# Two attention layers with state-space layers between: last stage of the kernels' transform on 32x32 tiles, loads and weights' loads moved

## The chip, the cores and the metric

One core of a Trainium2 chip. The metric is the device time of one execution in microseconds (us). Engines: PE (TensorE, matmuls and transposes), DVE (VectorE), ACT (ScalarE), POOL (GpSimd), SP (SyncE, which here issues most DMAs). Each engine runs its instructions in the order in which they stand.

## The reference

x has 2048 positions of 640 channels. Two pairs of layers, each behind a layer norm and added to x: attention with 32 heads of 20 channels, then a state-space layer whose long convolution is computed by FFT.

```python
def _A_ref(x, wqkv, wo):                      # attention
    q, k, v = qkv[0], qkv[1], qkv[2]
    p = _softmax(scores, axis=-1)
    ...
def _B_ref(u, log_A_real, A_imag, C_real, C_imag, log_dt, D_skip):
    K = 2.0 * jnp.einsum("dn,dnl->dl", C, P).real
    Kf = jnp.fft.rfft(K, L2)
    Uf = jnp.fft.rfft(u_t, L2)
    y = jnp.fft.irfft(Uf * Kf[None, :, :], L2)[:, :, :L]
    return y + u * D_skip[None, None, :]
```

K does not depend on x. Both state-space layers use the same K, so its transform is made once.

## The kernel before, in words

The program runs in this order: K is computed on the chip and written to DRAM (tensor kd); attention 1; its output projection, with the transform of K among it; state-space layer 1; attention 2; its output projection; state-space layer 2.

**Kernels' transform** (`ktransform`, lines 1029 to 1090). Five units of 128 channels. A unit does this:

1. DMA of kl (128 channels x 2048 positions, 1 MB) on SP; DVE adds the skip weight to one column (kl<-kl,skip).
2. 16 transposes by PE (pkt<-ident,kl, line 1053), four to a PSUM tile; four copies to ktr, half on DVE and half on ACT.
3. 32 fp32 matmuls of 128x128 (pkx<-ktr,e, line 1061; two PE instructions each in the trace), four to a PSUM tile; eight copies to kx1, half on DVE and half on ACT.
4. Eight steps q: four transposes (pkt<-ident,kx, line 1070), one copy by ACT to kxt (two buffers), then, one step behind, one fp32 matmul of 128x512 (pkf<-kxt,f, line 1078, two instructions in the trace). DVE shuffles partitions of pkf into kn0 and into kn1 (STREAM_SHUFFLE kn<-pkf), ACT scales kn1 by sgn. After two steps SP stores kn0 to kha and kn1 to khb, 128x1024 floats each. kn0 and kn1 have one buffer each.

PSUM in this stage: tags T, F, X and mm with two banks each.

**Output projection** (`out_proj`, lines 1092 to 1112). 16 groups s of 128 positions. A group loads otl, casts it to oh (ACT), subtracts to get ol (DVE), and runs 30 matmuls of 128x320 (po, lines 1098 and 1104), after which DVE adds po to x in two halves (x<-x,po) and the layer norm's steps follow. In program order, `weave(1000)` at s == 2 puts the whole transform there; a scheduler then decides how the instructions of the groups and of the transform lie among each other on every engine.

**State-space layer** (from line 1163): psx, pst, psv, psy on PE; ka and kb are loaded from kha and khb, 256 KB each.

**Attention.** For a group g of four heads, a block qb of 512 queries and a step kt of 128 keys, PE makes scores S (line 824), ACT takes the exponential (pt<-S), PE multiplies with V (pa, line 841). Beside it, the projections to q and k of the blocks of later heads run (line 578 and others): `fetch` loads their weights (DMA ws on SP), DVE and ACT empty the results, and SP stores them to DRAM as qs and ks. Loads of kop and qop bring them back for each group; for the next group they are issued at qb == 3, kt == 10. How much projection work must be done by which wave of attention is set by the table AHEAD; a planner (`slot`, `need`) places it.

Of the kernel before, what the change touches and what calls it, by code (L numbers as in the profile page):

```python
# [11 lines left out]
F32 = mybir.dt.float32  # L12
# [72 lines left out]
def mha_s4d_kernel(ctx, tc, x_in, wqkv, wo, lar, aim, cr, ci, ldt, dsk,  # L85
# [29 lines left out]
    kha = dram.tile([P, D // 4, P], F32, name="kha")  # L115
    khb = dram.tile([P, D // 4, P], F32, name="khb")
# [277 lines left out]
    def attention(x, stats):  # L394
# [162 lines left out]
        def jobs():  # L557
# [372 lines left out]
        for g in range(H // 4):  # L930
            need(NEED[g], ("v", g // 2))
            for qb in range(4):
                if g == H // 4 - 1 and qb == 3:
                    if tail is None:
                        need(*every)
                        tail = end_jobs()
                    split, fetch = out_split(tail[-1], 1 if first_layer else 2)
                    first = []
                    later.extend(((plan.pe + 7.0, fetch), (plan.pe + 20.0, lambda: first.append(split(0)))))
                    later.sort(key=lambda e: e[0])  # L940
                pa = [pst("A", [P, 512], F32, tag=f"pa{r}", name=f"pa{r}") for r in range(2)]
                for kt in range(NI):
                    kc, pts = P * (kt % 8), []
                    for j in range(2):
                        pts.append(scores(kop[j][kt // 8], kc, qop[j][qb % 2]))
                        if j:
                            ready.append((plan.act, qb, g, kt, pts, pa))
                        fill(j)
                    if kt == 2:
                        for j in range(2):  # L950
                            if qb == 0:
                                load_k(g, j, 1)
                            if qb < 3:
# [69 lines left out]
    DUP0 = list(range(16)) * 2  # L1023
    DUP1 = list(range(16, 32)) * 2

    def by_channel(x1, i2):
        return x1[:, :, i2].rearrange("p g (s c) -> p s g c", c=4)
# [1 line left out]
    def ktransform():  # L1029

        c = ExitStack()
        c1 = c.enter_context(tc.tile_pool(name="f1", bufs=1))
        c2 = c.enter_context(tc.tile_pool(name="f2", bufs=2))
        e1 = c1.tile([P, NI, 2, P], F32, name="e1")
        sy.dma_start(e1, c_e1.rearrange("p (i r k) -> p i r k", i=NI, r=2))
        f2 = c1.tile([P, P], F32, name="f2")
        sy.dma_start(f2, c_f2)
        sgn = c1.tile([P, 1], F32, name="sgn")
        sy.dma_start(sgn, c_sg)

        skip = c1.tile([P, NCT], F32, name="skip")
        sy.dma_start(skip, dsk)

        def unit_load(b):
            kl = c1.tile([P, L], F32, name="kl")
            sy.dma_start(kl, kd[b * P:b * P + P, :])
            ve.tensor_add(kl[:, 0:1], kl[:, 0:1], skip[:, b:b + 1])
            kt = c1.tile([P, NI, P], F32, name="ktr")
# [7 lines left out]
            x1 = c1.tile([P, 32, NI // 2, 16], F32, name="kx1")  # L1056
            for i2 in range(NI // 2):
                ps = pst("X", [P, 2, 2, P], F32, tag="X", name="pkx")
                for r in range(2):
                    for i in range(2):  # L1060
                        te.matmul(ps[:, r, i, :], e1[:, 2 * i2 + i, r, :], kt[:, 2 * i2 + i, :],
                                  start=True, stop=True)
                (ve.tensor_copy if i2 % 2 else se.copy)(by_channel(x1, i2), ps.rearrange("p r i (g c) -> p (r i) g c", c=4))
                yield
            prev = None
            for q in range(9):
                if q < 8:
                    pt = pst("T", [P, 4, P], F32, tag="T", name="pkt")
# [4 lines left out]
                if prev is not None:  # L1073
                    g0 = b * 32 + 4 * (q - 1)
                    if q % 2:
                        kn = [c1.tile([P, 2, 512], F32, name=f"kn{s}") for s in range(2)]
                    px = pst("F", [P, 512], F32, tag="F", name="pkf")
                    te.matmul(px, f2, prev, start=True, stop=True)  # L1078
# [7 lines left out]
                prev = xt  # L1086
                yield
        for b in range(NCT):
            yield from unit_load(b)
        c.close()  # L1090

    def out_proj(x, woh, wol, split, first, ln):
# [35 lines left out]
    def ssm(x, uh, ul, consts, last):  # L1128
# [19 lines left out]
        with ExitStack() as c:  # L1148
# [29 lines left out]
            def stage2b(b, q, xt):  # L1178
                g0 = b * 32 + 4 * q
                ka = c3.tile([P, 512], F32, name="ka")  # L1180
                kb = c3.tile([P, 512], F32, name="kb")
                sy.dma_start(ka, kha[:, g0:g0 + 4, :].rearrange("p g k -> p (g k)"))
                sy.dma_start(kb, khb[:, g0:g0 + 4, :].rearrange("p g k -> p (g k)"))
# [163 lines left out]
    def seq(x, general):  # L1347

        stats = None
        for n in range(0, len(parts), 2):  # L1350
            with ExitStack() as c:
# [49 lines left out]
def _constants():  # L1401
# [12 lines left out]
        f2[r, :, :, :, o] = np.einsum("ihl,cd->ichld", m.reshape(16, 4, 4), e4)  # L1414
    for s, o, m in ((0, 0, C), (1, 0, S), (0, 1, -S), (1, 1, C)):
        fa[:, s, :, :, o] = np.einsum("hli,cd->hlcid", m.reshape(4, 4, 16), e4)
    f2 = f2.reshape(2, NI // 2, 2, 4, P).transpose(1, 0, 2, 3, 4)
    sg = np.zeros((4, 2, 16, 1))
    sg[:, 0], sg[:, 1] = -1.0, 1.0
# [5 lines left out]
    cs = dict(c_e1=e1.reshape(P, -1), c_eb=eb.reshape(P, -1), c_f2=f2.reshape(P, P), c_sg=sg.reshape(P, 1),  # L1425
              c_fa=fa.reshape(P, -1), c_sel=sel.reshape(P, -1), c_lv=lv, c_id=np.eye(P))
    cs = {n: np.ascontiguousarray(a.astype(np.float32)) for n, a in cs.items()}
    for n, a in (("c_e16", e1), ("c_f16", f2)):
# [41 lines left out]
```

## Time and profile before

| what | value |
|---|---|
| median of 3 runs | 2717.64 us (2716.63 to 2720.64) |
| profiled execution | 2718.84 us |
| its span | 2717.1 us |
| mean granted TensorE clock | 0.991 |
| PE, DVE, ACT, POOL busy | 2534.4, 1477.0, 2337.4, 852.6 us |

A page of the profile gives busy time per engine, the chain of work that ended last, and groups of instructions: line, engine, operation, out<-in, shape, count, then busy time and mean ns of one, then the engine's idle time before them and what ended it. In timelines the columns are start, duration, engine, line, operation, and in brackets the idle time before it with its releaser. A row of windows gives the stretch, its length, and busy time with count for PE, PE's weight loads, DVE, ACT, POOL, then the clock, the share of DMA and GB/s. In the rows of a tile, "590/592/697" are the shortest, median and longest duration in ns, followed by the first and last start.

### The profile page before, as it was taken

The numbers are of one execution on the slowest core, as the hardware profiler recorded it, in microseconds if no ns is written. First come the engines' busy times: TensorE is split into PE (matmuls) and PEld (weight loads), VectorE is DVE, ScalarE is ACT, GpSimd is POOL, SyncE is SP. The second block draws the span as 40 slices with busy tenths as digits, with TensorE's granted clock in tenths as the row PEclk, the third lists the DMA queues.
The fourth block names the chain that finished last, engine by engine and source line by source line (L and its number), as shares of the span: only waits on it lengthen the run. The fifth ranks groups of instructions, "written<-read, shape, count | busy, mean of one in ns | idle before, by whom it ended". The sixth has DMA issues, their size and how long they took to land.

```text
span 2717.1 us, 115609 instructions
## 1 busy us (share of the span) xinstructions
PE 2534.4 (93%) x50944; PEld 1445.2 (53%) x50944; DVE 1477.0 (54%) x3292; ACT 2337.4 (86%) x2762; POOL 852.6 (31%) x1282
## 2 busy tenths in 40 slices
PE   7899999999999988999999999899999998888998
PEld 3445444444444433777886445444445443335988
DVE  7777877778856970577776332232232220003865
ACT  7899999999999999455655899899999999997464
POOL 1132333333333343301670122222223223222376
PEclk9999999999999999999999999999999999999999
DMA  6522222232222232455542111111121112112365
GB/s 214 174 62 75 63 77 64 73 75 61 65 51 59 51 112 87 145 210 194 178 142 67 45 52 52 50 53 46 46 66 35 50 36 61 41 38 80 110 191 161
DMA packets 183153, 238.55 MB, mean 88 GB/s; under 512 B 42737, under 2 KB 128241, under 8 KB 180849
## 3 DMA queue, kind: packets, MB, share of 16 engines
q1 hardware_dynamic: 146304, 184.48, 21.0%
q0 software_dynamic: 36336, 46.59, 7.2%
q8 instruction: 402, 6.59, 1.0%
q14 instruction: 111, 0.90, 0.1%
HBM read 154.90 MB, written 76.03 MB: 85 GB/s over the span
## 4 chain that ended last, share of the span: by engine, by line
ACT 49%; PE 30%; issue 9%; DVE 7%; DMA 4%; POOL 1%; SPq 0%; ACTq 0%; DVEq 0%; POOLq 0%
ACT pt L77 47%; PE pa L841 5%; PE S L824 3%; PE psv L1198 3%; PE po L1104 3%; PE psy L1208 2%; PE m L578 2%; PE psx L1186 2%; PE psx L1163 2%; PE po L1098 1%; PE pst L1173 1%; PE pkf L1078 1%; DMA kop<-ks 1%; PE pv L544 1%; PE pq L730 1%
## 5 line engine op out<-in xcount | busy, mean ns | idle before, releaser
L77 ACT ACTIVATE pt<-S 128x1024 f32<-128x1024 f32 x2048 | 1922.9, 1037 | 46.7 <-PE S L824 37.1
L841 PE MATMUL pa<-pt,V 64*32 64x512 f32 x16384 | 1101.0, 590 | 0.9 <-DVE oc L77 0.8
L824 PE MATMUL S<-qop,kop 61*32 61x512 f16 x16384 | 880.4, 381 | 125.4 <-ACT pt L77 105.1
L824 PEld LDWEIGHTS <-kop 61*32 61x32 f16 x16384 | 375.1, 89 | 784.1 <-issue 660.0
L841 PEld LDWEIGHTS pa<-pt,V 64*32 64x32 f32 x16384 | 315.0, 106 | 69.9 <-DVE oc L77 6.6
L77 POOL DMA_DIRECT2D dn<-oc x256 | 126.7, 501 | 700.9 <-DVE oc L77 644.7
L77 DVE COPY oc<-pa 128x512 f32<-128x512 f32 x64 | 44.2, 690 | 312.1 <-PE pa L841 307.2
L77 DVE TENSOR_SCALAR qc<-m 128x512 f32<-128x512 f32 (+1 forms) x68 | 46.9, 689 | 296.4 <-PE m L578 296.4
L77 POOL DMA_DIRECT2D db<-dn x256 | 130.0, 513 | 111.6 <-DMA dn<-dr 107.7
L578 PE MATMUL m<-xh,wh 64*32 64x512 f16 x2560 | 146.7, 379 | 1.4 <-DVE qc L77 1.4
L578 PE MATMUL m<-xh,wl 64*32 64x512 f16 x2560 | 147.3, 378 | 0.0
L578 PE MATMUL m<-xl,wh 64*32 64x512 f16 x2560 | 145.5, 377 | 0.0
L77 POOL DMA_DIRECT2D ot<-oc x256 | 130.2, 516 | 12.7 <-issue 8.3
L578 PEld LDWEIGHTS <-wh 64*32 64x32 f16 x5120 | 92.5, 94 | 74.1 <-issue 32.6
L1191 POOL TENSOR_TENSOR t<-t,kb 128x512 f32<-128x512 f32 x80 | 102.0, 1276 | 72.3 <-DVE t L77 58.2
L77 ACT COPY xt<-pst 128x1024 f16<-128x1024 f16 x80 | 81.5, 1022 | 47.6 <-PE pst L1173 47.5
L77 POOL DMA_DIRECT2D dn<-dr x64 | 35.8, 559 | 257.5 <-DVE dr L77 237.1
L544 PEld LDWEIGHTS <-xh 128*128 128x128 f16 x960 | 79.6, 98 | 50.9 <-issue 35.6
L77 DVE TENSOR_TENSOR kb<-ktab 128x512 f32<-128x512 f32 x160 | 106.3, 682 | 0.0
L77 DVE TENSOR_SCALAR V<-m 128x160 f32<-128x160 f32 x64 | 20.7, 324 | 156.3 <-PE m L544 156.3
L77 DVE TENSOR_SCALAR dr<-dr 128x16 f32<-128x16 f32 x64 | 11.0, 171 | 171.8 <-DMA dr<-dn 171.6
L1020 POOL TENSOR_TENSOR ul<-u,uh 128x640 f16<-128x640 f32 x30 | 46.1, 1555 | 177.7 <-ACT uh L77 177.7
(269 smaller groups left out, 4045.7 us busy)
## 6 DMA issues: line engine op xcount, KB each, us to landing
ka<-kha SPq DMA_DIRECT2D x80, 256.0 KB
kb<-khb SPq DMA_DIRECT2D x80, 256.0 KB
db<-dn POOLq DMA_DIRECT2D x256, 64.0 KB, 2.7
kpw<-wd POOLq DMA_DIRECT2D x60, 192.0 KB, 4.8
qop<-qs SPq DMA_DIRECT2D x256, 40.0 KB
kop<-ks SPq DMA_DIRECT2D x128, 80.0 KB
ot<-oc POOLq DMA_DIRECT2D x256, 40.0 KB, 2.3
otl<-ot SPq DMA_DIRECT2D x32, 320.0 KB
```

The source lines that it names most:

```text
L77: made = f(out, *a, **k)
L544: chain(te.matmul(ps[:, :n], a_[:, ct, sl], m[:, ct, :], start=(k == 0), stop=(k == 14)))
L578: chain(te.matmul(ps[r][32 * t:32 * t + 32, :], a_[rows, ct, 32 * u:32 * u + 32], m[rows, ct, 512 * v:512 * v + 512], start=(k == 0), stop ...
L824: chain(te.matmul(S[32 * t:32 * t + 32, 512 * r:512 * r + 512], kt_[rows, kc + 32 * t:kc + 32 * t + 32], qt[rows, :], start=True, stop=Tru ...
L841: chain(te.matmul(pa[r][32 * j:32 * j + 32, :], V[rows, kt, VP * h:VP * h + 32], pts[j // 2][rows, 512 * (j % 2):512 * (j % 2) + 512], sta ...
L1020: (ve if s == NI - 1 else ge).tensor_sub(ul[:, s, :], u, uh[:, s, :])
L1104: te.matmul(pos[hf], oh[:, ct, :], m[:, ct, 320 * hf:320 * hf + 320], start=False, stop=(ct == NCT - 1 and m is wol))
L1163: te.matmul(ps[:, r, i, :], e1[:, e, s, r, :], m[:, s, bs], start=(n == 0), stop=(n == 2))
L1186: te.matmul(px, f2[:, f, :], xt[:, k, :], start=(n == 0), stop=(n == 2))
L1191: ge.tensor_mul(t2, t2, kb)
L1198: te.matmul(pv[:, g].rearrange("p r i c -> p (r i c)"), t1[:, g * P:g * P + P], fa, start=True, stop=True)
L1208: te.matmul(py[:, i, :], eb[:, 4 * i4 + i, r, :], v[:, r, 4 * i4 + i].rearrange("p g c -> p (g c)"), start=(r == 0), stop=(r == 1))
```

## The change

In the transform's last stage a unit now has two halves t. A half makes 16 transposes and four copies (kxt, one buffer of 128x4x4x128), then 16 matmuls on 32x32 tiles, each 32x512 (pkf, now line 1083): tile row ch, tile column g, into four PSUM tags F0 to F3 of one bank each. Then, for each ch, shuffles and scaling as before; after two ch, kn0 and kn1 are stored by four DMAs each, of 32x8x128 floats. f2 has 32 columns, kx1 and kha/khb other layouts. ktr's copies all go to ACT, and six of eight kx copies. pkt moves to tag X. The load of the next unit's kl is issued ahead of the last stage. In attention, `fetch` takes up one weights' load a unit later, a job for V has an empty first step, AHEAD has smaller numbers from its third entry on, and the next group's loads stand at kt == 8.

```diff
-AHEAD = ((0, 0.0), (110, 6.0), (236, 34.0), (364, 61.0), (600, 95.0), (740, 134.0))
+AHEAD = ((0, 0.0), (110, 6.0), (236, 32.0), (364, 59.0), (600, 93.0), (740, 130.0))
...
-                if order and (order[0][0] == "v" or not ws_):
+                elif order and (order[0][0] == "v" or not ws_):
...
             def vq(q):
+                yield 0.0, 0.0, False, ()
...
-                    if qb == 3 and kt == 10 and g + 1 < H // 4:
+                    if qb == 3 and kt == 8 and g + 1 < H // 4:
...
-        def unit_load(b):
+        def load(b):
             kl = c1.tile([P, L], F32, name="kl")
             sy.dma_start(kl, kd[b * P:b * P + P, :])
+            return kl
+
+        def unit_load(b, kl):
...
-                pt = pst("T", [P, 4, P], F32, tag="T", name="pkt")
+                pt = pst("X", [P, 4, P], F32, tag="X", name="pkt")
...
-                (se.copy if i4 % 2 else ve.tensor_copy)(kt[:, 4 * i4:4 * i4 + 4, :], pt)
+                se.copy(kt[:, 4 * i4:4 * i4 + 4, :], pt)
...
-                (ve.tensor_copy if i2 % 2 else se.copy)(by_channel(x1, i2), ps.rearrange("p r i (g c) -> p (r i) g c", c=4))
+                (ve.tensor_copy if i2 % 4 == 3 else se.copy)(
+                    x1[:, :, :, i2, :].rearrange("p g c s -> p s g c"), ps.rearrange("p r i (g c) -> p (r i) g c", c=4))
...
+            if b + 1 < NCT:
+                kls.append(load(b + 1))
+            for t in range(2):
+                xt = c1.tile([P, 4, 4, P], F32, name="kxt")
+                for q in range(4):
+                    pt = pst("X", [P, 4, P], F32, tag="X", name="pkt")
                     for g in range(4):
-                        te.transpose(pt[:, g, :], x1[:, 4 * q + g].rearrange("p i s -> p (i s)"), ident)
-                    xt = c2.tile([P, 512], F32, name="kxt")
-                    se.copy(xt, pt.rearrange("p g k -> p (g k)"))
...
-                    px = pst("F", [P, 512], F32, tag="F", name="pkf")
-                    te.matmul(px, f2, prev, start=True, stop=True)
...
+                        te.transpose(pt[:, g, :], x1[:, 16 * t + 4 * q + g].rearrange("p c i s -> p (c i s)"), ident)
+                    se.copy(xt[:, q], pt)
+                px = [pst("F", [P, 512], F32, tag=f"F{ch}", name=f"pkf{ch}") for ch in range(4)]
+                for ch in range(4):
+                    rows = slice(32 * ch, 32 * ch + 32)
+                    for g in range(4):
+                        te.matmul(px[ch][32 * g:32 * g + 32, :].rearrange("p (q k) -> p q k", k=P), f2[rows, :],
+                                  xt[rows, :, g, :], start=True, stop=True, tile_position=(32 * ch, 32 * g))
+                for ch in range(4):
+                    if ch % 2 == 0:
                         kn = [c1.tile([P, 2, 512], F32, name=f"kn{s}") for s in range(2)]
                     for s in range(2):
-                        ve.stream_shuffle(kn[s][:, (q - 1) % 2, :], px, [DUP0, DUP1][s])
-                    se.activation(kn[1][:, (q - 1) % 2, :], kn[1][:, (q - 1) % 2, :], AF.Copy, scale=sgn)
-                    if q % 2 == 0:
+                        ve.stream_shuffle(kn[s][:, ch % 2, :], px[ch], [KDUP0, KDUP1][s])
+                    se.activation(kn[1][:, ch % 2, :], kn[1][:, ch % 2, :], AF.Copy, scale=sgn)
+                    if ch % 2:
                         for s, dst in enumerate((kha, khb)):
-                            sy.dma_start(dst[:, g0 - 4:g0 + 4, :].rearrange("p g k -> p (g k)"),
-                                         kn[s].rearrange("p q k -> p (q k)"))
+                            for g in range(4):
+                                sy.dma_start(
+                                    dst[2 * b + t].rearrange("(a c) q g k -> g a (c q) k", c=4)[g][:, 4 * ch - 4:4 * ch + 4],
+                                    kn[s][32 * g:32 * g + 32].rearrange("p c (q k) -> p (c q) k", k=P))
...
-                    psum(c3, M=2, T=2, F=2)
+                    psum(c3, M=2, F=1)
```

**DVE in the middle of the transform.** Where the fourth unit's copies kx1 stand, before; kn0 and kn1 are of the third unit, kl of the fifth:

```order
L77 STREAM_SHUFFLE kn0_27170<-pkf_27172 128x512
L77 STREAM_SHUFFLE kn0_27170<-pkf_27177 128x512
L77 COPY kx1_27212<-pkx_27219 128x4x32x4
L77 TENSOR_TENSOR kl_27373<-kl_27373,skip_26615 128x1
L77 COPY kx1_27212<-pkx_27231 128x4x32x4
L77 STREAM_SHUFFLE kn1_27171<-pkf_27172 128x512
L77 STREAM_SHUFFLE kn1_27171<-pkf_27177 128x512
L77 COPY kx1_27212<-pkx_27243 128x4x32x4
```

and now, where pair 2 of the third unit writes kn0_27216 and kn1_27217, the copies kx1_27335 are the fourth unit's, and pairs 3 and 4 follow:

```order
L77 TENSOR_TENSOR kl_27153<-kl_27153,skip_26612 128x1
L77 STREAM_SHUFFLE kn0_27216<-pkf2_27182 128x512
L77 STREAM_SHUFFLE kn0_27216<-pkf3_27183 128x512
L77 COPY kx1_27335<-pkx_27354 128x4x128
L77 COPY kx1_27335<-pkx_27378 128x4x128
L77 STREAM_SHUFFLE kn1_27217<-pkf2_27182 128x512
L77 STREAM_SHUFFLE kn1_27217<-pkf3_27183 128x512
L77 STREAM_SHUFFLE kn0_27277<-pkf0_27257 128x512
L77 STREAM_SHUFFLE kn0_27277<-pkf1_27258 128x512
```

The add to the fourth unit's kl and both of its kx copies on DVE now stand ahead of the kn1 shuffles of pair 2, and so of pairs 3 and 4; before, the four kx copies stood among the shuffles of the last pair.

**SP in the middle and at the end of the transform.** Before, stores of the third unit's pairs, with the fifth unit's load of kl and a load of out-projection among them:

```order
L77 DMA kha<-kn_27142 128x1024
L77 DMA kl<-kd 128x2048
L77 DMA khb<-kn_27143 128x1024
L77 DMA kha<-kn_27170 128x1024
L77 DMA khb<-kn_27171 128x1024
L77 DMA otl<-ot 128x5x128
L77 DMA kha<-kn_27275 128x1024
```

and now, the last pair of the second unit, the load of the fourth unit's kl, and the first pair of the third unit; further down the last pair of all:

```order
L77 DMA kha<-kn_27062 32x8x128 x4
L77 DMA khb<-kn_27063 32x8x128 x4
L77 DMA kl<-kd 128x2048
L77 DMA kha<-kn_27200 32x8x128 x4
L77 DMA khb<-kn_27201 32x8x128 x4
...
L77 DMA kha<-kn_27753 32x8x128 x4
L77 DMA khb<-kn_27754 32x8x128 x4
L77 DMA otl<-ot 128x5x128 x4
L77 DMA ka<-kha 128x512
```

The load of kl now stands behind all stores of a unit, and the last four loads otl stand behind all stores; on PE the 120 matmuls of the last four groups of out-projection stand behind the last pkf, where before its groups lay among the transform to the end.

**SP in attention 2,** at a change of the group of heads: before and now, the weights' loads ws, the stores qs of a projection, and the first loads kop and qop of the next group.

```order
L77 DMA ws<-in_wqkv 128x5x128
L77 DMA ws<-in_wqkv 128x5x160
L77 DMA qs<-qhi 128x512
L77 DMA qs<-qlo 128x512
L77 DMA kop_30504<-ks 40x1x1024
L77 DMA kop_30504<-ks 20x1024
```

```order
L77 DMA ws<-in_wqkv 128x5x128
L77 DMA kop_30710<-ks 40x1x1024
L77 DMA kop_30710<-ks 20x1024
...
L77 DMA qop_30716<-qm 1x512
L77 DMA qs<-qhi 128x512
L77 DMA qs<-qlo 128x512
L77 DMA ws<-in_wqkv 128x5x160
```

One pair of qs stores and one load of weights moved from ahead of the group's loads to behind them.

More of the change, by code (lines that the diff above doesn't have):

```diff
@@ L114, in mha_s4d_kernel @@
     wd = dram.tile([P, 3, len(LV), D], F32, name="wd")
-    kha = dram.tile([P, D // 4, P], F32, name="kha")
-    khb = dram.tile([P, D // 4, P], F32, name="khb")
+    kha = dram.tile([2 * NCT, P, 4, 4, P], F32, name="kha")
+    khb = dram.tile([2 * NCT, P, 4, 4, P], F32, name="khb")
     qs = dram.tile([2, D, L], F16, name="qs")
@@ L1022, in mha_s4d_kernel @@
     SWAP = list(range(16, 32)) + list(range(16))
-    DUP0 = list(range(16)) * 2
-    DUP1 = list(range(16, 32)) * 2
+    KDUP0 = [8 * (n // 8) + n % 4 for n in range(32)]
+    KDUP1 = [n + 4 for n in KDUP0]
     def by_channel(x1, i2):
@@ L1035, in ktransform @@
         sy.dma_start(e1, c_e1.rearrange("p (i r k) -> p i r k", i=NI, r=2))
-        f2 = c1.tile([P, P], F32, name="f2")
+        f2 = c1.tile([P, 32], F32, name="f2")
         sy.dma_start(f2, c_f2)
@@ L1050, in unit_load @@
             for i4 in range(4):
-                pt = pst("T", [P, 4, P], F32, tag="T", name="pkt")
+                pt = pst("X", [P, 4, P], F32, tag="X", name="pkt")
                 for i in range(4):
                     te.transpose(pt[:, i, :], klv[:, 4 * i4 + i, :], ident)
-                (se.copy if i4 % 2 else ve.tensor_copy)(kt[:, 4 * i4:4 * i4 + 4, :], pt)
+                se.copy(kt[:, 4 * i4:4 * i4 + 4, :], pt)
                 yield
-            x1 = c1.tile([P, 32, NI // 2, 16], F32, name="kx1")
+            x1 = c1.tile([P, 32, 4, NI // 2, 4], F32, name="kx1")
             for i2 in range(NI // 2):
@@ L1087, in unit_load @@
                 yield
+        kls = [load(0)]
         for b in range(NCT):
-            yield from unit_load(b)
+            yield from unit_load(b, kls.pop())
         c.close()
@@ L1181, in stage2b @@
                 kb = c3.tile([P, 512], F32, name="kb")
-                sy.dma_start(ka, kha[:, g0:g0 + 4, :].rearrange("p g k -> p (g k)"))
-                sy.dma_start(kb, khb[:, g0:g0 + 4, :].rearrange("p g k -> p (g k)"))
+                sy.dma_start(ka, kha[g0 // 16, :, q % 4].rearrange("p g k -> p (g k)"))
+                sy.dma_start(kb, khb[g0 // 16, :, q % 4].rearrange("p g k -> p (g k)"))
                 px = pst("F", [P, 512], F32, tag="F", name="psx")
@@ L1416, in _constants @@
         fa[:, s, :, :, o] = np.einsum("hli,cd->hlcid", m.reshape(4, 4, 16), e4)
+    k2 = f2[:, :, 0, :, :, :, 0].reshape(2, NI // 2, 2, 32).transpose(1, 0, 2, 3).reshape(1, 32, 32)
+    k2 = np.repeat(k2, 4, axis=0)
     f2 = f2.reshape(2, NI // 2, 2, 4, P).transpose(1, 0, 2, 3, 4)
-    sg = np.zeros((4, 2, 16, 1))
-    sg[:, 0], sg[:, 1] = -1.0, 1.0
+    sg = np.zeros((4, 4, 2, 4, 1))
+    sg[:, :, 0], sg[:, :, 1] = -1.0, 1.0
     sel = np.zeros((P, NBLK, H))
@@ L1424, in _constants @@
     lv = np.array(LV)[None, :]
-    cs = dict(c_e1=e1.reshape(P, -1), c_eb=eb.reshape(P, -1), c_f2=f2.reshape(P, P), c_sg=sg.reshape(P, 1),
+    cs = dict(c_e1=e1.reshape(P, -1), c_eb=eb.reshape(P, -1), c_f2=k2.reshape(P, 32), c_sg=sg.reshape(P, 1),
               c_fa=fa.reshape(P, -1), c_sel=sel.reshape(P, -1), c_lv=lv, c_id=np.eye(P))
```

8 lines of the change are left out of this document (removed).

## The prediction, made before the result was known

> **What bounds the kernel now.** I read the page first, then windows by stage, then the groups of single tiles, then timelines and the chain of waits at the places that the change touches.
>
> ```profile
> span 2717.1 us, 115609 instructions
> ACT 49%; PE 30%; issue 9%; DVE 7%; DMA 4%; POOL 1%; SPq 0%; ACTq 0%; DVEq 0%; POOLq 0%
> L77 ACT ACTIVATE pt<-S 128x1024 f32<-128x1024 f32 x2048 | 1922.9, 1037 | 46.7 <-PE S L824 37.1
> ```
>
> The profiled execution took 2718.84 us around a span of 2717.1; the sum below starts from 2718.84, 1.2 above the median of 2717.64. Attention, about half of the chain, is ScalarE's exponentials: only 46.7 us of idle time stand before 1922.9 us of them. The change's main part lies elsewhere, in the stage between layer 1's attention and the state-space layer:
>
> ```profile
> 1140.00:1285.00 145.00, 141.68 (x917) 114.52 (x918) 104.68 (x283) 76.84 (x131) 11.15 (x8) 1.00 0.49 188
> L77 DVE STREAM_SHUFFLE kn<-pkf x80: 724/737/761, 1154.6 to 1283.1; 128x512 f32<-128x512 f32 x80
> L77 ACT ACTIVATE kn<-kn,sgn x40: 706/722/730, 1156.0 to 1283.8; 128x512 f32<-128x512 f32 x40
> 1136.81 2.95 PE po L1104 x20
> 1162.87 1.76 PE pkf L1078 x4
> ```
>
> In the window's row PE is busy for 141.68 of 145 us, DVE for 104.68, ACT for 76.84. So TensorE bounds this stage as it stands: out-projection groups (30 matmuls; 2.95 / 20 = 0.147 each, so 4.4 us) fill every hole that the kernels' transform leaves. From the first shuffle to the last the five units take (1283.1 + 0.7 − 1154.6) / 5 = 25.8 us each.
>
> **The change part by part.** *Last matmuls.* Four pkf instructions take 1.76 us, 0.44 each; a unit has 16, or 7.0 us. Now there are 32 tile matmuls per unit; if each is two instructions as before, 64. The nearest row for small tiles is attention's 64x32 one:
>
> ```profile
> L841 PE MATMUL pa<-pt,V 64*32 64x512 f32 x16384 | 1101.0, 590 | 0.9 <-DVE oc L77 0.8
> ```
>
> 1101.0 / 16384 = 67 ns apiece of engine time although one lasts 590: 4.3 us for 64. Twice as many tiles fit with 32x32, so 34 to 67 ns bound it (2.2 to 4.3 us); serial, at 0.44, would be 28 us. PE's gain is 2.7 to 4.8 us per unit, 13 to 24 in five, **if TensorE stays the bound**. The program's order says it doesn't.
>
> *Output ring.* kn0 and kn1 have one buffer each. A timeline of before shows a pair of steps go round:
>
> ```profile
> 1210.36 0.74 DVE L77 STREAM_SHUFFLE kn<-pkf 128x512 f32<-128x512 f32 x1
> 1210.48 0.32 SPq L77 DMA_DIRECT2D kha<-kn  x1
> 1211.13 0.72 ACT L77 ACTIVATE kn<-kn,sgn 128x512 f32<-128x512 f32 x1
> 1211.87 0.32 SPq L77 DMA_DIRECT2D khb<-kn  x1
> 1213.24 0.01 DVE L77 LOAD_MASK_SELECT kn<-pkf  x1 [2.15 <-DMA kha<-kn]
> 1756.03 2.30 SPq L77 DMA_DIRECT2D kop<-ks  x4
> ```
>
> From kha's issue to the next write of kn0 it is 2.76 us, 2.44 of it after the issue. Ring of kn1 now: two shuffles (1.37), the last scaling by sgn (0.8 with its hand-over), one issue (0.32), 2.44: 4.9 us. Changed: four issues, between 4 × 0.32 = 1.28 and the 2.30 of four kop loads; I take 1.4, near the plain store's row. The tail has a quarter of the bytes behind its last issue; between 2.0 and 2.44, I take 2.1. Ring: 1.37 + 0.8 + 1.4 + 2.1 = **5.7 us**, 22.7 for the four pairs of a unit. So by this alone DVE's share of a unit is below 25.8.
>
> A rule of the Trainium skill speaks against the eight small stores: DMA: Bandwidth & Descriptors, Rules for kernel authors, tells authors to coalesce many small transfers into one, and the same page has a fixed 2.0 us in every transfer plus its bytes at 436 GB/s. By that, an estimate, the tail would be 2.3 us instead of 2.1 and the ring 5.9, 4 us more over twenty pairs; its 3.2 us for 512 KB stands against the trace's 2.76.
>
> *The wait added to the ring.* In the changed order the two kx copies on DVE of the **next** unit stand between the second pair's kn0 and kn1 shuffles, all of kn1's later work behind them; and on SP the load of kl for the unit after stands behind all 32 stores of the unit before it. So "ahead" means one stage ahead in the code, but in SP's order the load is issued with the last khb of the preceding unit. What follows a kl load:
>
> ```profile
> 1222.27 6.22 DMA kl<-kd
> 1140.72 0.14 DVE L77 TENSOR_TENSOR kl<-kl,skip 128x1 f32<-128x1 f32 x1
> 1143.60 7.68 PE pkx L1061 x64
> 1151.32 0.69 DVE L77 COPY kx<-pkx 128x512 f32<-128x512 f32 x1 [1.18 <-PE pkx L1061]
> L77 ACT COPY ktr<-pkt x10: 565/587/589, 1142.1 to 1250.4; 128x512 f32<-128x512 f32 x10
> L77 DVE COPY ktr<-pkt x10: 671/684/693, 1141.7 to 1250.1; 128x512 f32<-128x512 f32 x10
> ```
>
> 6.2 us from issue to the add, then 1151.32 + 0.69 − 1140.72 = 11.3 to the last kx copy. With ktr's four copies all on ACT (4 × 0.587 in a row, not two engines side by side) I add 0.4, bounds 0 and 1.2: 11.7. The scattered writes of kx (pieces of 4 bytes) have no row; I leave the 0.59 and 0.69 us of the copies, bounds 0 and, copy for copy doubled, +5 per unit on ACT. After it come the second pair's kn1 half, then two rings: 2 × 5.67 + 1.37 + 0.8 + 1.4 = 14.9 to the last khb issue, which lets the next kl go. A unit: 6.2 + 11.7 + 14.9 = **32.8 us**, against 25.8. In before nothing of the kind holds: kl is issued between stores and kx copies go where PE has them.
>
> A second rule, of TensorEngine Tiling (Array Packing), PSUM Bottleneck: tiling makes TensorE faster but not the emptying of PSUM, which may become the bottleneck. The 16 shuffles of 737 ns per unit stay as they were, and the trace agrees: 11.8 us of DVE per unit outlast either price of the tile matmuls. By that rule alone none of PE's 13 to 24 us would reach the end; by PE's busy row all of them.
>
> *Where out-projection goes.* Its groups no longer lie beside units 3 to 5: after the last pkf stand four whole groups, and their loads otl behind the last khb.
>
> ```profile
> 1154.64 0.73 DVE L77 STREAM_SHUFFLE kn<-pkf 128x512 f32<-128x512 f32 x1
> 1283.07 0.73 DVE L77 STREAM_SHUFFLE kn<-pkf 128x512 f32<-128x512 f32 x1
> 1283.76 0.47 DVE L77 TENSOR_TENSOR x<-x,po 128x320 f32<-128x320 f32 x1
> L77 SPq DMA_DIRECT2D otl<-ot x32: 359/360/683, 1048.9 to 2543.1; - x32
> L77 DVE TENSOR_TENSOR ol<-otl,oh x32: 806/823/1114, 1079.9 to 2551.1; 128x640 fp32r<-128x640 f32 x32
> L77 ACT CAST oh<-otl x30: 708/727/732, 1077.1 to 2550.2; 128x640 fp32r<-128x640 f32 x30
> ```
>
> Time line of the changed stage. Four transposed groups and 16 tiles instead of one group precede the first shuffle: 1158 instead of 1154.6. Pair 1 ends at 1160.8; kl of unit 2 is in early, but its transposes stand behind pair 1's buffers: kx done at about 1172. The rest of unit 1 takes 14.9 us, and its pairs 3 and 4 stand on DVE behind x additions of three out-projection groups (13.2 us of PE, about 8 of it not covered): last khb at about 1195. Units 2, 3 and 4: 3 × 32.8, to 1293.4. Unit 5 has no kx to wait for: 22.7, to 1316. Then otl 0.36 + 2.44 (kha's tail), oh 0.73, ol 0.82, four groups 17.6, the add 0.5: **1338.5** where before has 1283.76 + 0.47 = 1284.2. The state-space part follows as it did. Stage: **+54 us**, bounds +30 (cheap issues, no uncovered groups, kl in 5.9) to +75 (2.3 us for four stores, scattered copies dear).
>
> *Attention.* Loads at step 8 instead of 10, weights a unit later, AHEAD 2 to 4 us less:
>
> ```profile
> 1751.78 1.02 ACT L77 ACTIVATE pt<-S 128x1024 f32<-128x1024 f32 x1 [2.83 <-PE S L824]
> 1758.22 1.02 ACT L77 ACTIVATE pt<-S 128x1024 f32<-128x1024 f32 x1 [5.42 <-PE S L824]
> 2127.92 8.03 ACT L77 ACTIVATE pt<-S 128x1024 f32<-128x1024 f32 x8 [2.57 <-PE S L824]
> 1740.43 1.32 SPq L77 DMA_DIRECT2D qs<-qhi  x1
> ```
>
> In layer 2 ACT stands for 2.83 + 5.42 us where the next group's kop and qop loads were issued behind a projection's store qs at 1740.43; in the changed order ws and then the loads come first, and qs after. 2.57 more belong to a like place at 2127.9. At most 10.8 us go. The projection work that now comes later may crowd another gap, so I take **−8**, bounds −11 and +3.
>
> *At nothing:* pkt in the X pool (its two banks are part of the 11.7); f2 of 32 columns; the ka and kb loads, still one 256 KB transfer each.
>
> Sum: 2718.84 + 54.3 − 8 = **2765**.
>
> **Rivals.** *The kx wait is hidden* (kl lands early enough, or DVE has its copies before pair 2): then only the ring holds, 20 × 5.67 = 113 from 1158, plus 7 uncovered in unit 1, plus 22.5 for the tail: 1301, +17; with −8, 2728. Against it: a load that SP issues only after the stores can't land before them. *TensorE stays the bound* (faster): DVE and SP keep pace with it, out-projection fills holes as before, and PE's 13 to 24 us are gained: with −8 that is 2687 to 2698, taken 2692. For it speaks 141.68 of 145 us; it decides if a unit of DVE's chain is under about 22 us, and the chain above is 32.8. *Stores or tiles dearer:* four small stores at the 2.30 of the kop row add 0.9 per ring, 13 rings in line: 2777; tiles that run one after another need 28 us per unit on PE, 42 with the rest, and 5 × (42 − 32.8) more: 2811. Against: the 67 ns above. *The change doesn't do what it says:* the load "ahead" isn't ahead in SP's order; that is my forecast itself.
>
> **How the numbers follow.** A difference under 0.2% (5.4 us) is one that a measurement of this kernel can't tell from none. Forecast 0.64, 2745 to 2785 by the bounds; ring alone 0.12, 2722 to 2740; dearer 0.08, 2785 to 2811; TensorE bound 0.12, 2687 to 2700; no change 0.04. Faster 0.12, same 0.04, slower 0.84. The range from 2720 to 2795 leaves out the faster case and the far end of the dear one.
>
> **What would show it.** Windows over units 3 to 5: PE busy for half or less, and DVE idle before its kx copies, ended by PE pkx, about 10 us per unit; kl's issue right behind the last khb of a unit; first shuffles of units 32 to 33 us apart; 17.6 us of po alone after the last shuffle; ACT's 5.42 us at the group change gone. I am wrong if PE stays above 90% busy there, if kl's issue precedes the stores, if a unit takes under 26 us, or if four stores take over 2 us on SP.

## The result, and the profile after

The changed kernel takes **2794.38 us** (median of 4 runs, 2791.38 to 2797.47) against 2717.18 of the kernel before: ratio 1.0281, 95% interval 1.0264 to 1.0299. The prediction was 2765, with a range from 2720 to 2795: the side and the mechanism came as forecast, the size was 29 us short. 2794.38 lies 0.6 us inside the stated range, and outside the 2745 to 2785 that the prediction gave to its own case; two of the four runs lie above 2795. The profiled execution took 2791.62 us around a span of 2789.7, 72.8 more than the profiled one of before.

The page of the changed kernel: span, the busy shares and the granted clock in 40 slices, and the exponentials.

```profile
span 2789.7 us, 116284 instructions
PE   7899999999998988877699999999999998888998
PEclk9999999999999999977799999999999999999999
L77 ACT ACTIVATE pt<-S 128x1024 f32<-128x1024 f32 x2048 | 1922.1, 1038 | 38.6 <-PE S L825 28.6
```

Slices 17 to 19 (counted from 0), about 1190 to 1400 us, are where PE is less busy and its clock lower. Windows from the last exponential of attention 1 to the last addition of out-projection, of the changed kernel and then of the kernel before (columns: stretch, length, busy time and count of PE, its weight loads, DVE, ACT, POOL, then clock, DMA share, GB/s):

```profile
1102.20:1375.00 272.80, 200.07 (x1398) 153.64 (x1397) 128.96 (x337) 113.09 (x171) 30.00 (x33) 0.82 0.51 131
```

```profile
1099.80:1284.30 184.50, 178.86 (x1159) 149.20 (x1158) 134.45 (x354) 86.69 (x147) 29.53 (x32) 1.00 0.52 192
```

The stage grew by 88.3 us. TensorE was idle for 5.6 of its 184.5 us; now it is idle for 72.7 of 272.8. One unit of the changed kernel, from one load of kl to the next, as the chain of waits tells it:

```profile
1249.24 5.96 DMA kl<-kd
1255.22 0.17 DVE kl L77
...
1255.48 3.61 PE pkt L1057 x16
...
1260.24 1.05 ACT kx L77
...
1265.92 2.09 PE pkx L1065 x16
...
1268.90 0.79 DVE kn L77 x2
1269.71 1.37 ACT kn L77 x2
...
1272.46 2.65 DMA khb<-kn
...
1278.86 2.61 DMA khb<-kn
...
1285.22 0.47 SPq L77
...
1285.79 6.15 DMA kl<-kd
```

This is the loop of the forecast: kl, its add, transposes, the eight pkx groups with their copies, only then the kn1 shuffles of the second pair, two more rings, and the next kl behind the last khb store. It takes 1285.79 − 1249.24 = 36.55 us, where 32.8 were forecast and 25.8 were the unit's time before. The end of the stage on SP:

```profile
1345.74 1.83 SPq L77 DMA_DIRECT2D khb<-kn  x4
1347.62 9.92 SPq L77 DMA_DIRECT2D otl<-ot  x4
1373.66 0.34 SPq L77 DMA_DIRECT2D ka<-kha  x1
```

The four loads for out-projection stand behind the last store, and its four groups run alone until 1375. The chain of waits there, and the windows of units 3 and 4, of the last unit and of the four groups:

```profile
1347.62 3.92 DMA otl<-ot
...
1353.20 3.03 PE po L1109 x10
...
1359.93 1.58 PE po L1109 x10
```

```profile
1249.30:1285.80 36.50, 24.77 (x177) 15.68 (x175) 13.04 (x35) 17.77 (x27) 0.00 (x0) 0.78 0.58 143
1285.80:1322.50 36.70, 26.25 (x176) 16.33 (x176) 13.04 (x35) 18.05 (x27) 0.00 (x0) 0.73 0.59 144
1322.50:1347.60 25.10, 8.12 (x64) 4.75 (x64) 9.62 (x28) 7.09 (x12) 0.00 (x0) 0.57 0.73 167
1347.60:1375.00 27.40, 20.42 (x120) 19.77 (x121) 15.10 (x37) 5.96 (x11) 3.28 (x3) 0.81 0.23 63
```

TensorE is busy for 68 to 72% of units 3 and 4, for a third of the last one, and its granted clock falls with it, to 0.57.

In attention 2 the waits of 2.83 and 5.42 us at the group change are gone. The first loads kop for it are issued 227.2 us after the first exponential (at 1816.55), where it was 238.8 (at 1742.33), and the wait that is left there is 0.49 us:

```profile
1839.84 1.02 ACT L77 ACTIVATE pt<-S 128x1024 f32<-128x1024 f32 x1 [0.49 <-PE S L825]
```

Its first and last rows of exponentials in the changed kernel, then in the kernel before:

```profile
1589.37 2.85 ACT L77 ACTIVATE pt<-S 128x1024 f32<-128x1024 f32 x3 [4.14 <-PE S L825]
2555.48 3.83 ACT L77 ACTIVATE pt<-S 128x1024 f32<-128x1024 f32 x4
```

```profile
1503.50 2.85 ACT L77 ACTIVATE pt<-S 128x1024 f32<-128x1024 f32 x3 [4.31 <-PE S L824]
2481.66 3.84 ACT L77 ACTIVATE pt<-S 128x1024 f32<-128x1024 f32 x4
```

2559.3 − 1589.4 = 969.9 us against 2485.5 − 1503.5 = 982.0. The account of the 72.6 us of span: attention 1 ends 2.4 later, the stage takes 88.3 more, the state-space layer 1 to the first exponential 4.9 less, attention 2 12.0 less, the rest 1.2 less.

### The profile page after: what moved, and what is told of

Its sections match the earlier page's. It is cut to its first block, busy times and chain, and to the rows that moved or that the text cites. A ratio compares the mean times of both kernels' runs of the same rounds, so it can differ in the third digit from the quotient of the medians.

```text
span 2789.7 us, 116284 instructions
## 1 busy us (share of the span) xinstructions
PE 2545.1 (91%) x51184; PEld 1440.4 (52%) x51184; DVE 1469.4 (53%) x3272; ACT 2361.1 (85%) x2782; POOL 849.6 (30%) x1282
## 4 chain that ended last, share of the span: by engine, by line
ACT 50%; PE 25%; issue 9%; DVE 8%; DMA 5%; SPq 1%; POOL 1%; DVEq 0%; ACTq 0%; POOLq 0%
ACT pt L77 46%; PE pa L842 4%; PE psv L1209 3%; PE po L1115 3%; PE psy L1219 2%; PE S L825 2%; PE psx L1197 2%; PE psx L1174 1%; PE m L578 1%; PE po L1109 1%; PE pst L1184 1%; SPq L77 1%; PE pkx L1065 1%; DMA khb<-kn 1%; DVE ktab L77 1%
## 5 line engine op out<-in xcount | busy, mean ns | idle before, releaser
L1203 POOL TENSOR_TENSOR t<-t,t 128x512 f32<-128x512 f32 x78 | 99.1, 1271 | 8.5 <-DVE t L77 2.6
```

Source lines behind the costliest of these rows:

```text
L1203: (ge if g0 else ve).tensor_add(t1, t1, t2)
```

## The experiments

Times are medians; ratios are to the kernel before on the same chip, with their 95% interval. "Single store" means that one DMA stores a pair.

**1. Attention edits alone.** The kernel before with these lines:

```diff
-AHEAD = ((0, 0.0), (110, 6.0), (236, 34.0), (364, 61.0), (600, 95.0), (740, 134.0))
+AHEAD = ((0, 0.0), (110, 6.0), (236, 32.0), (364, 59.0), (600, 93.0), (740, 130.0))
...
-                if order and (order[0][0] == "v" or not ws_):
+                elif order and (order[0][0] == "v" or not ws_):
...
+                yield 0.0, 0.0, False, ()
...
-                    if qb == 3 and kt == 10 and g + 1 < H // 4:
+                    if qb == 3 and kt == 8 and g + 1 < H // 4:
```

> The kernel before with only the four edits in attention: the weights' load a unit later, the dummy first step, the smaller AHEAD, the next group's loads at step 8. The transform is that of before. Theory: attention 2 is shorter by about 12 us, attention 1 longer by about 2.5, as in the trace of the changed kernel: near 2708 us, 2705 to 2712. Rival: those 12 us came from the shifted start and the idle clock and not from these edits: 2717.

2709.71 us, 0.9968 (0.9957 to 0.998). The gain is real without the transform's change. Attention 2 lasts 971.6 us, 10.4 less; attention 1 lasts 990.1 instead of 984.3, with a wait that the kernel before does not have, the same one as in the changed kernel (row of this run):

```profile
852.79 3.02 ACT L77 ACTIVATE pt<-S 128x1024 f32<-128x1024 f32 x3 [4.70 <-PE S L825]
```

**2. Transform alone.** The changed kernel with those lines as they were.

```diff
-AHEAD = ((0, 0.0), (110, 6.0), (236, 32.0), (364, 59.0), (600, 93.0), (740, 130.0))
+AHEAD = ((0, 0.0), (110, 6.0), (236, 34.0), (364, 61.0), (600, 95.0), (740, 134.0))
...
-                elif order and (order[0][0] == "v" or not ws_):
+                if order and (order[0][0] == "v" or not ws_):
...
-                yield 0.0, 0.0, False, ()
...
-                    if qb == 3 and kt == 8 and g + 1 < H // 4:
+                    if qb == 3 and kt == 10 and g + 1 < H // 4:
```

> The changed kernel with the four edits in attention undone; only the transform is new. Theory: the terms add up, so it lacks the 8 to 12 us that attention gives: near 2804 us. Rival as for the attention run: 2794, no difference.

2804.76 us, 1.0323 (1.0306 to 1.034). The parts nearly add up: 7.2 less by the first run and 87.9 more by this one are 80.7, against 77.2 together. The waits of attention 2 are back:

```profile
1836.88 1.02 ACT L77 ACTIVATE pt<-S 128x1024 f32<-128x1024 f32 x1 [2.58 <-PE S L824]
1843.02 1.02 ACT L77 ACTIVATE pt<-S 128x1024 f32<-128x1024 f32 x1 [5.12 <-PE S L824]
```

Attention 1 has no wait of 4.70 here and yet lasts 988.9 us: some 4 us of difference in that layer come without the edits too.

**3. Single stores in the changed kernel.**

```diff
-    kha = dram.tile([2 * NCT, P, 4, 4, P], F32, name="kha")
+    kha = dram.tile([2 * NCT, 4, 32, 16, P], F32, name="kha")
...
-                            for g in range(4):
-                                sy.dma_start(
-                                    dst[2 * b + t].rearrange("(a c) q g k -> g a (c q) k", c=4)[g][:, 4 * ch - 4:4 * ch + 4],
-                                    kn[s][32 * g:32 * g + 32].rearrange("p c (q k) -> p (c q) k", k=P))
+                            sy.dma_start(dst[2 * b + t].rearrange("g a m k -> (g a) (m k)")[:, 512 * ch - 512:512 * ch + 512],
+                                         kn[s].rearrange("p c f -> p (c f)"))
...
-                sy.dma_start(ka, kha[g0 // 16, :, q % 4].rearrange("p g k -> p (g k)"))
...
+                sy.dma_start(ka.rearrange("p (g k) -> p g k", k=P), kha[g0 // 16].rearrange("g a (c q) k -> q (a c) g k", q=4)[q % 4])
...
```

> The changed kernel with kha and khb laid out so that one DMA of 128x1024 floats stores a pair, as in the kernel before; the loads ka and kb read pieces of 512 bytes instead. Tile matmuls, kx copies, copies on ACT and the load ahead stay. In its program order out-projection lies among all five units again and the second pair's shuffles no longer stand behind the next unit's kx copies. Theory (the eight stores set the order, and the order makes the stage long): the stage ends near that of before, TensorE bound, attention gives its 10: 2695 to 2720 us, near 2705. Rival (the prices of the operations make it long: kx copies of 1.04 us instead of 0.59 and 0.69, tile matmuls, all copies on ACT): the stage stays 40 us or more above before, 2750 or more.

2723.26 us, 1.0021 (1.0011 to 1.0031): 71 us of the loss are gone with the eight stores, though tiles, kx copies and copies on ACT all stayed. Its window from attention 1 to the last addition:

```profile
1107.00:1302.30 195.30, 171.84 (x1398) 143.28 (x1397) 124.84 (x333) 109.40 (x169) 28.55 (x32) 0.97 0.52 183
```

195.3 us instead of 272.8, the clock back to 0.97. The 512-byte pieces of ka and kb cost nothing to be seen: the state-space layer takes no longer than before (217.7 us to attention 2's first exponential against 219.3).

**4. Four stores for each one, in the kernel before.** No tile matmul, no other edit:

```diff
-                            sy.dma_start(dst[:, g0 - 4:g0 + 4, :].rearrange("p g k -> p (g k)"),
-                                         kn[s].rearrange("p q k -> p (q k)"))
+                            for g in range(4):
+                                sy.dma_start(dst[32 * g:32 * g + 32, g0 - 4:g0 + 4, :],
+                                             kn[s][32 * g:32 * g + 32].rearrange("p q (g k) -> p (q g) k", k=P))
```

> The kernel before with each store of a pair cut into four DMAs of 32 partitions (same layout, same bytes, pieces of 4 KB), nothing else. In its program order the kx copies of the next unit stand ahead of whole units' shuffles and groups of out-projection move together. Theory (number of stores sets the order): the stage grows by 30 to 70 us, near 2765. Rival (small stores cost only their issue): ring 1.4 us longer for 20 pairs, much of it beside other work: 2720 to 2740.

2787.01 us, 1.0264 (1.0247 to 1.0281): 70 us, nearly the whole loss, from cutting each store into four alone. Timeline of this run, on SP and on PE:

```profile
1210.86 1.70 SPq L77 DMA_DIRECT2D kha<-kn  x4
1214.26 1.70 SPq L77 DMA_DIRECT2D khb<-kn  x4
1216.05 0.37 SPq L77 DMA_DIRECT2D kl<-kd  x1
1216.47 7.95 SPq L77 DMA_DIRECT2D otl<-ot  x3
```

```profile
1221.49 3.00 PE L1053 MATMUL pkt<-ident,kl 128*128 128x128 f32 x12 [11.84 <-DVE kl L77]
```

Here too the scheduler put kl and the loads of out-projection behind all stores of two units, and TensorE waits 11.84 us for kl with no group of out-projection to do. The same wait comes once more, 11.86 us before 1306.29. What the split costs is the new order and the longer issue (four in 1.70 us instead of one in 0.32) together; the run doesn't part the two. An estimate: a pair's ring has one group of four in line, so the issue alone adds at most 20 × 1.4 = 28 us, and the two waits for kl alone are 23.7 us in which TensorE is idle.

**5. kx copies in another order of elements.** The changed kernel; the write has runs of 16 bytes again, the read of PSUM steps by 512 bytes.

```diff
-                    x1[:, :, :, i2, :].rearrange("p g c s -> p s g c"), ps.rearrange("p r i (g c) -> p (r i) g c", c=4))
+                    x1[:, :, :, i2, :].rearrange("p g c s -> p (g c) s"), ps.rearrange("p r i d -> p d (r i)"))
```

> The changed kernel; only the kx copies walk the same elements in another order, so that they write runs of 16 bytes again and read PSUM at a step of 512 bytes. The program order on DVE is that of the changed kernel. Theory: scattered writes made a copy 1.04 us, so it falls back to about 0.59 (ACT) and 0.69 (DVE); the chain from kl's add to the last kx copy loses about 2 us per unit, 5 units, 8 to 12 us: near 2784. Rival (a strided read of PSUM costs as much as a scattered write): copies stay at 1.04 us, 2794.

2789.08 us, 1.0264 (1.0247 to 1.0281). Copies of the changed kernel, then of this run:

```profile
L77 ACT COPY kx<-pkx x30: 1035/1042/1093, 1149.8 to 1304.1; 128x512 f32<-128x512 f32 x30
L77 DVE COPY kx<-pkx x10: 1011/1046/1092, 1153.6 to 1305.0; 128x512 f32<-128x512 f32 x10
```

```profile
L77 ACT COPY kx<-pkx x30: 586/586/598, 1151.7 to 1301.2; 128x512 f32<-128x512 f32 x30
L77 DVE COPY kx<-pkx x10: 690/692/692, 1154.7 to 1302.2; 128x512 f32<-128x512 f32 x10
```

The copies fall as expected, 0.46 and 0.35 us each; the kernel gains about half of the 10 us expected: 5.3 by the medians, and in the traces the stage takes 267.4 us instead of 272.8. The two ratios' intervals overlap.

**6. Single stores and the swapped copies together** (edits of 3 and 5).

> One store per pair as in the earlier run (2723 us) and the kx copies in the swapped order. Theory: there TensorE waits for kx and kxt copies; if a copy falls to about 0.6 us, the 11 us by which the stage was longer than before go, and the tiles' gain of 4.7 us per unit shows in part: 2700 to 2712. Rival: copies stay at 1.05 us, 2723.

2713.66 us, 0.9981 (0.9969 to 0.9992): 9.6 below run 3, just above the range: the copies' part came, the tiles' part did not. Here the tiles cost what the bounds of the prediction allowed (2.2 to 4.3 us per unit): all 320 pkf instructions take TensorE 17.34 us, 3.5 per unit, against 40.27 for 80 full ones in the kernel before. But the stage isn't shorter than before. Its window, then that of pkf alone (PE, weight loads, DVE), then PE's longest group of waits (us in total, times, longest):

```profile
1102.70:1294.10 191.40, 169.88 (x1399) 144.99 (x1398) 121.81 (x333) 97.55 (x169) 28.59 (x32) 0.96 0.53 187
1148.00:1298.00 150.00, 17.34 (x320) 3.37 (x320) 54.57 (x160) 0.94 0.53 190
```

```profile
PE pkt L1077 <- ACT kxt L77: 12.0, 5, 2.5
```

In the changed kernel itself the price was another: the same 320 instructions took 37.22 us, hardly less than the full ones. They come there in groups of 16 behind waits for the shuffles of the PSUM tiles, and at a lower clock (0.79 in this window). The changed kernel, then the kernel before:

```profile
1144.00:1375.00 231.00, 37.22 (x320) 6.30 (x320) 54.70 (x160) 0.79 0.49 119
1140.00:1285.00 145.00, 40.27 (x80) 12.87 (x80) 54.94 (x160) 1.00 0.49 188
```

The transposes pkt of the stage (PE, weight loads, DVE where it has any, ACT), in run 6 and then before:

```profile
1102.70:1294.10 191.40, 41.77 (x240) 31.79 (x240) 33.39 (x60) 0.96 0.53 187
1099.80:1284.30 184.50, 35.38 (x240) 28.89 (x240) 6.83 (x10) 28.46 (x50) 1.00 0.52 192
```

**7. As 6, copies of ktr and kx by halves on ACT and DVE.**

```diff
-                se.copy(kt[:, 4 * i4:4 * i4 + 4, :], pt)
+                (se.copy if i4 % 2 else ve.tensor_copy)(kt[:, 4 * i4:4 * i4 + 4, :], pt)
...
-                (ve.tensor_copy if i2 % 4 == 3 else se.copy)(
+                (ve.tensor_copy if i2 % 2 else se.copy)(
```

> As the run before it in this call, with the copies of ktr and kx shared between ACT and DVE by halves as in the kernel before. Theory (ACT, with all ktr copies, six kx copies, kxt and sgn, holds TensorE up): a few us less than the run before it, 2695 to 2708. Rival (DVE's shuffles are then late): a few us more.

2715.44 us, 0.9992 (0.9983 to 1.0002): no gain. ACT's share of these copies alone does not hold the stage up; TensorE still waits 12.3 us for kxt.

**8. Single stores, the load of kl not ahead.**

```diff
-            if b + 1 < NCT:
-                kls.append(load(b + 1))
...
-        kls = [load(0)]
         for b in range(NCT):
-            yield from unit_load(b, kls.pop())
+            yield from unit_load(b, load(b))
```

> One store per pair, with the load of the next unit's kl issued at its unit's start as before, not ahead of the last stage. The order on DVE is the same as with the load ahead. Theory (kl has one buffer and SP's queue decides, so the load ahead gains nothing): within 3 us of 2723. Rival (the load ahead hides 6 us of transfer per unit): 2735 to 2750.

2722.8 us, 1.0011 (1.0001 to 1.0021), run 3 without the load ahead: the same. With single stores, the load "ahead" is worth nothing that can be measured. With eight small stores it was not tried apart.

**9. As 6, kn0 and kn1 per step with two buffers each** (same space, one 128x512 DMA per step).

```diff
-                        kn = [c1.tile([P, 2, 512], F32, name=f"kn{s}") for s in range(2)]
+                    kn = [c2.tile([P, 512], F32, name=f"kn{s}") for s in range(2)]
...
```

> One store per pair's half: kn0 and kn1 hold one step and have two buffers each in the same space, with one DMA of 128x512 per step (16 a unit), kx copies in swapped order. Theory (with the single store the ring of kn still bounds a unit at 4 times about 5 us beside kx, so that TensorE's gain cannot show): the ring is loosened, TensorE waits less, 2690 to 2708. Rival (the number of stores alone matters, 16 a unit being twice the 8): slower than 2713.7 by 10 or more.

2715.97 us, 0.9984 (0.9975 to 0.9993). The theory failed here: a looser ring does not let TensorE's gain through. 16 stores per unit on SP, each of 256 KB from 128 partitions, did not do what the changed kernel's 32 of 128 KB from 32 partitions do either; whether it is their number or their shape was not tried apart.

**10. As 1, with the same two buffers for kn0 and kn1.**

> The kernel with only the attention edits (2709.7) and the same two buffers per step for kn0 and kn1, full 128x128 matmuls as before. Theory (there TensorE bounds the stage, 141 of 144 us, so a looser ring gains nothing): 2706 to 2712. Rival (the ring bounds it too): 2700 or less.

2712.79 us, 0.997 (0.9959 to 0.9982), as without them. With full matmuls the ring is not the bound.

**11. The changed kernel, khb's stores from POOL's queue.**

```diff
-                                sy.dma_start(
+                                (ge if s else sy).dma_start(
```

> The changed kernel with the four small stores of khb issued from POOL's queue, those of kha from SP's. In its program order units 1 to 3 have out-projection beside them again, units 4 and 5 are without kx or out-projection at the end. Theory (the count of small stores in one queue sets the order): between the changed kernel and the one with single stores, 2735 to 2770. Rival (number of stores, wherever issued): 2785 to 2795.

2777.28 us, 1.021 (1.0194 to 1.0226), 17 below the changed kernel and above the forecast. Out-projection ends at 1246.7 there, but the last units run alone until 1361: half of the small stores moved to another queue don't bring the order of single stores back. The run changes the stores' price as well: one takes 0.58 us on POOL's queue, and DVE waits 61.2 us in all for landings of khb.

**12. Attention edits in layer 2 alone,** the rest as before.

```diff
+AHEAD2 = ((0, 0.0), (110, 6.0), (236, 32.0), (364, 59.0), (600, 93.0), (740, 130.0))
...
+                if (first_layer or not had) and order and (order[0][0] == "v" or not ws_):
...
+                if not first_layer:
+                    yield 0.0, 0.0, False, ()
...
+            tab = AHEAD if first_layer else AHEAD2
...
+                    if qb == 3 and kt == (10 if first_layer else 8) and g + 1 < H // 4:
```

> The kernel before with the four edits in attention in layer 2 alone; layer 1 and the transform are those of before. Theory (the edits shorten attention 2 by about 12 us by clearing its waits for S, and cost attention 1 about 5 us by a wait of 4.7 us that they make): attention 1 as before without the wait of 4.7, attention 2 at 970 us: 2703 to 2707. Rival (attention 1's difference is only scatter between programs): 2709 to 2712, as with the edits in both layers.

**2706.18 us**, 0.9955 (0.994 to 0.9971), the lowest of all, though its interval overlaps that of run 1 (0.9957 to 0.998). Attention 1 lasts 984.2 us as in the kernel before (984.3), without the wait of 4.70; attention 2 lasts 972.0. The wait goes with the edits in layer 1, then; that leaving them out there makes the kernel faster is likely but not shown, as attention 1 took 988.9 us in run 2 without edits.

## Why the prediction was right, and where its sizes were off

- **The side and the loop: right.** The second pair's kn1 shuffles waited for the next unit's kx copies, kl for the last store, and out-projection ran alone at the end. Unit 5, which has no next unit's kx to wait for, agrees inside one trace: 25.1 us (1322.5 to 1347.6), where units 2 to 4 take 37.4 on average.
- **The size: within the range by luck.** The stage came out 90.8 us later than before (1375.0 against 1284.2), above the bounds of +30 to +75. The time still fell 0.6 us inside the range because other parts gained more than forecast. From 2765 to the profiled 2791.62: the stage +36.5, attention 2 −4.0 (−12.0 for −8), the state-space layer −4.9, the rest −1.2.
- **The signs named beforehand: not all came.** TensorE was busy for 68 to 72% of units 3 and 4, not half or less; first shuffles lie 36.7 to 39.4 us apart, not 32 to 33; and of the 40 groups of four stores 18 took over 2 us on SP (up to 3.16), which was named as a sign of being wrong. The rival "stores dearer" thus holds in part; kl behind the last khb and the 5.42 us came as said.
- **The cause of the order: argued then, tested now.** The prediction took the order as given. Runs 3 and 4 show that splitting the stores makes it, with the longer issue that comes with it: without the split the changed kernel loses 71 us of its 77, with it the kernel before grows by 70. Why the scheduler turns the order over no run here shows.
- **kx copies: mis-sized.** Left at 0.59 and 0.69 with a doubling only as a bound; they took 1.04 and 1.05. Run 5 prices this at 5 us.
- **Ring: mis-sized.** Forecast 5.7 us, four issues at 1.4 and a tail of 2.1. In the trace of the unit above it is 6.4 (1271.10 to 1277.50, khb to khb): the four issues take 1.82, within their bounds, and the tail behind them 2.44 (1272.92 to the shuffle at 1275.36), its dear end. Over the 13 rings in line that is 9.5 us, a part of what follows.
- **Unit: 32.8 forecast, 37.4 on average measured,** 14 us over three; the rest of the first unit took 9.5 more than allowed, the first shuffle came 3.4 later, the last unit took 2.4 more, and the tail 27.4 instead of 22.5. With the 2.4 by which attention 1 ended later that makes 36.5 us: 1338.5 was forecast and 1375 came.
- **Tail: mis-sized.** otl landed 3.9 us after its issue, not 2.8. The first ten po took 3.03 us behind 18.77 us of idle time, at a granted clock of 0.50; the first ten of the second group took 1.58.
- **Attention: right,** −9.6 in the trace (−12.0 in attention 2, +2.4 in attention 1) for −8 forecast, and −7.2 by itself. Which of the four edits does it was not tried apart.
- **State-space layer 1** gained 4.9 us that the sum did not have. TensorE is busy there for 201.53 us instead of 205.02, with no fewer instructions (2000 and 1993), at a clock of 0.99 instead of 0.96; why the clock differs is open.
- **The rival "TensorE stays the bound"** has the tile price that the forecast bounded, but only with the order repaired (run 6): 17.34 us for 320 instructions, 54 ns each, between 34 and 67. In the changed kernel it is 37.22, 116 ns each. And even in run 6 the stage takes 191.4 us against 184.5. TensorE's busy time fell by 9 us and not by 23: the transposes pkt take 41.77 us instead of 35.38, and the full pkf had lain over their neighbours more (the times of pkf, pkx, pkt and po add up to 20.9 us over the busy time before, 13.6 in run 6; pkx and po take nearly the same in both). It also waited 21.5 us, 12 of them for kxt copies. Neither ACT's share of the copies (run 7) nor the ring (run 9) removes that wait. One buffer of kxt per half is a cause that is left; that was not tried.

The Trainium skill's rule on small transfers (DMA: Bandwidth & Descriptors, Rules for kernel authors), weighed in the prediction, held: splitting the stores cost 70 us in run 4. The tail after the last issue was 2.44 us by the trace where the Trainium skill's figures, which that page gives for DMAs issued from GpSimd, gave an estimate of 2.3. So most of the loss is not in this tail.

A doubt that stays: the lower clock, 0.73 to 0.78 in units 3 and 4. Part of the loop's 36.55 us is matmuls that run at it. That the clock follows the idle time, and not the other way, is argued from run 3, where another order on the queues brought it back to 0.97 with the same matmuls; no run took the clock alone away.

## What to carry to other kernels

When an engine's program is put in order by a scheduler, a cheaper instruction elsewhere is worth what that order makes of it: read where the new waits stand on each queue before adding up prices, and look at the number of DMAs on a queue first. Cutting one store into four cost 70 us here; the tile matmuls beside it saved 23 us of one instruction group's time at best (run 6) and 3 in the changed kernel. Test each part of a bundled change alone: the attention edits are 7 us faster than the kernel that they were built on, and the tiles, with their stores and copies mended, added nothing to that (0.9981 in run 6, 0.9968 without them in run 1).

## What the runs showed of the hardware

- A copy of 128x512 floats that writes single 4-byte elements 128 bytes apart takes 1.04 us, and 0.586 (ACT) or 0.692 (DVE) when it writes runs of 16 bytes; reading PSUM at a step of 512 bytes instead costs nothing (run 5). The Trainium skill states lines of 16 bytes in SBUF (SBUF — State Buffer, Door 1: The DMA port swizzle), with a penalty for each access that crosses to a new line; the run agrees, though it doesn't show the size of a line.
- A pkf instruction on a 32x32 tile lasts 600 ns (median of run 6), and yet 320 of them take 17.34 us of TensorE: they lie over each other.
- One store's issue on SP takes 0.32 us alone (kernel before); four small ones of khb mostly take 1.82 to 1.92 us in the changed kernel, those of kha up to 3.16, and mostly 1.70 in run 4.
- TensorE's granted clock fell to 0.57 in the last unit, where it was busy for 8.12 of 25.1 us, and was 0.97 when the order filled it again.
